# A fused transformer block on one core: first MLP's softplus as one table instruction, table sets in the planner, float32 products begun per head pair

## The chip, the cores and the metric

The kernel runs on 1 core of one Trainium2 chip. The time is the device time of one execution, in microseconds (us). Engines are named as in the profile: PE (TensorE matmul), PEld (its weight loads), DVE (VectorE), ACT (ScalarE), POOL (GpSimd), SP (SyncE, which issues the transfers).

## What is computed

Attention of q, k, v (4 batches, 8 heads, 576 rows, 64 columns), then two MLPs (512 to 2048 to 512) over all 2304 rows:

```python
out_d = sm_attn(q_d, k_d, v_d)                 # q, k, v averaged over 4 rows, 144 rows each
out_up = np.repeat(out_d, factor, axis=2)
mask = np.abs(pos[:, None] - pos[None, :]) < factor
attn = np.exp(scores); attn = attn / (np.sum(attn, axis=-1, keepdims=True) + 1e-09)
return (out_up + out_local).astype(np.float32)

h = x @ w_in                                   # first MLP
g = np.maximum(h, 0.0) + np.log1p(np.exp(-np.abs(h)))
return (g @ w_out).astype(np.float32)

h = x @ w_in                                   # second MLP
g = h * np.cos(h)
return (g @ w_out).astype(np.float32)
```

The weights arrive as float64. The first MLP's g is softplus(h).

## The kernel before

**Tiles.** Rows are cut into five token tiles, t = 0 to 4, of 512, 512, 512, 512 and 256 rows. The 2048 hidden columns are 16 features f of 128. Almost all products are float16 with three terms (high times high, high times low, low times high), so each operand is split into a high and a low half. Only tile 0 of the first MLP does its first F0 = 6 features otherwise: `first_in(f)` (from L1270) multiplies the float32 weights by the float32 attention output `raw0` .. `raw3` (one for each pair of heads, c = 0 to 3), at L1277; `first_out(f)` (L1300) multiplies the result by float32 w1o at L1314. Features 6 to 15 of tile 0 and all later tiles go through `unit_in` (L1327, matmuls at L1341), `rest_in` (L1424) and `l2` (matmuls at L1522). The second MLP's products stand at L1376 and L1572.

**Attention.** `pair(b, c)` (L739) does one batch and one pair of heads, sixteen in all. Its steps carry the names p<b><c> and a letter: sum1, sum2 (pooled q, k), sum3, sum4 (pooled v), A (scores), A2 and A3 (maximum, subtraction), A4 (exp, L852), B, B1, B1a, B2 (the same for the pooled scores; exps at L937), A5, N1, N2, A6, B4 (sums, reciprocals, scaling; B4 is one DVE instruction), C, C0, C1, D, D1 (transposes and their copies by ACT), E (products with v), up, E1 (the sum, written to `raw` or to `xt`).

**Weights.** `Weight.decode` (load, rebase by ACT L636 with Prelu, join1 and join2 by DVE L480 and L644), `bound` (ACT L666, Abs with an accumulator), `fit` (a maximum over partitions by a PE transpose and DVE) and `split` (high by ACT L495 or DVE, low by DVE L491) turn a block of two features into float16 halves.

**Softplus before.** Per unit of a feature: ACT takes Abs (L1438) and Relu (L1442) of the product in PSUM, Exp (L1446), Ln (L1450); DVE adds them (step G, L491), then step gh copies to float16 (ACT L501 or DVE L503) and step gl takes the rest (DVE L483). In `first_in` it is Abs, Exp, Ln (L1286, L1290, L1294) and the DVE step G (L1298).

**Order.** All steps are put in a `Plan`. `order()` runs a list scheduler over five queues: of the steps that are ready, the one due first goes to a free engine; due times come from a backward pass, plus the hand-fitted offsets of the table MOVES. Each engine then executes in exactly that order. Where the planner has no PE work it issues matmuls of zeros (`filler`, L1850), which keep PE running. PSUM is four two-bank slots (`any`); `halve(0, ...)` turns one of them into two one-bank slots `h`, which `first_in` and `unit_in` write to. In the kernel before it does so after the last of the first four pairs:

```python
        for b, c in pairs[:4]:
            pair(b, c)
...
        halve(0, outs_of[3:])
```

## Time and profile before

| | |
|---|---|
| median of 3 runs (lowest, highest) | 847.86 us (846.75 to 848.07) |
| span of the profiled execution | 847.6 us, 0.26 us below that median |
| PE busy | 834.0 us, 98% of the span |
| DVE busy | 719.1 us, 85% |
| ACT busy | 533.6 us, 63% |
| mean granted PE clock | 0.998 |
| HBM | 53.85 MB read, 4.72 MB written |

The profiled execution is told by its span alone, from its first to its last instruction. Busy times are averages over stages: what binds is read stage by stage, and PE counts as busy with its matmuls of zeros too. A duration in a row contains a tail that the next instruction of the engine overlaps; where work is added up, the distance from start to start is used.

### The profile page before, as it was taken

Reading aid. Unit: us, or ns where it says so; the run is one execution under the profiler, and the core shown is the slowest. Engines: PE = TensorE matmul, PEld = TensorE weight load, DVE = VectorE, ACT = ScalarE, POOL = GpSimd, SP = SyncE. Lnnn points to the kernel's source line nnn. Section 1 sums busy time; section 2 is a strip of 40 time slices with the busy share of each in tenths; the row PEclk is TensorE's granted clock in tenths of the full one; section 3 lists DMA queues with packets and bytes.
Section 4 is the critical chain, followed back from the end, with each engine's and each line's share of the span. In section 5 each row is a group of like instructions: output and inputs, shape, how many; then the busy total and the mean of one; then the engine's idle time right before and its main releaser. Section 6 shows DMA issues by size and latency. Waiting matters only on the chain.

```text
span 847.6 us, 15741 instructions
## 1 busy us (share of the span) xinstructions
PE 834.0 (98%) x6325; PEld 493.8 (58%) x6325; DVE 719.1 (85%) x1482; ACT 533.6 (63%) x964; POOL 1.8 (0%) x9
## 2 busy tenths in 40 slices
PE   8988999999999999999999999999999999999998
PEld 4634545455545555444467886676666565676664
DVE  7989999997767858999968999998779679889763
ACT  5478996686635747699977876556444335555441
POOL 0000000000000000000000000000000000000000
PEclk9999999999999999999999999999999999999999
DMA  9876441112110300342023200000000100100010
GB/s 321 281 277 240 162 173 41 51 33 64 61 45 1 117 1 2 120 178 100 1 99 107 94 2 1 1 1 29 23 1 1 51 1 1 51 1 2 2 50 25
DMA packets 14361, 59.57 MB, mean 70 GB/s; under 512 B 1681, under 2 KB 1809, under 8 KB 10193
## 3 DMA queue, kind: packets, MB, share of 16 engines
q1 hardware_dynamic: 14288, 58.58, 19.9%
q8 instruction: 49, 0.80, 0.4%
q14 instruction: 24, 0.19, 0.1%
HBM read 53.85 MB, written 4.72 MB: 69 GB/s over the span
## 4 chain that ended last, share of the span: by engine, by line
PE 89%; ACT 5%; DVE 3%; DMA 2%; issue 0%; POOL 0%; POOLq 0%; ACTq 0%; SPq 0%
PE any L1572 22%; PE h L1376 20%; PE any L1522 19%; PE h L1341 19%; PE any L1314 1%; PE any L1097 1%; PE any L1850 1%; DMA stg<-w1o 1%; PE any L817 1%; PE any L972 1%; PE h L1277 1%; DMA stg<-w1i 1%; ACT w1i_t L636 1%; ACT w1i_t L495 0%; DVE w1i_t L644 0%; ACT ed L937 0%
## 5 line engine op out<-in xcount | busy, mean ns | idle before, releaser
L1572 PE MATMUL any<-w1i_t,g 128*128 128x512 f16 x864 | 197.8, 379 | 0.5 <-DVE w1o_t L497 0.5
L1341 PE MATMUL h<-xt,w1i_t 128*128 128x512 f16 (+1 forms) x888 | 179.5, 356 | 0.1
L1376 PEld LDWEIGHTS <-w2i_t 128*128 128x128 f16 x1536 | 150.2, 98 | 31.6 <-issue 0.3
L1522 PE MATMUL any<-g,w1o_t 128*128 128x512 f16 (+1 forms) x792 | 157.2, 353 | 0.0
L1572 PEld LDWEIGHTS <-g 128*128 128x128 f16 x864 | 84.5, 98 | 88.4 <-issue 1.1
L1341 PEld LDWEIGHTS <-w1i_t 128*128 128x128 f16 x888 | 86.1, 98 | 83.0 <-issue 2.6
L1522 PEld LDWEIGHTS <-w1o_t 128*128 128x128 f16 x888 | 85.7, 98 | 79.9 <-issue 1.4
L483 DVE TENSOR_TENSOR g<-td,g 128x512 f16<-128x512 f32 (+1 forms) x146 | 92.0, 630 | 8.9 <-ACT g L501 6.0
L1376 PE MATMUL h<-xt,w2i_t 128*128 128x256 f16 x720 | 94.3, 273 | 0.1
L1474 ACT ACTIVATE tc<-ta 128x512 f32<-128x512 f32 (+1 forms) x80 | 46.8, 585 | 66.7 <-DVE ta L483 64.6
L1376 PE MATMUL h<-w1o_t,w2i_t 128*128 128x256 f16 x624 | 78.9, 273 | 0.0
L501 ACT ACTIVATE g<-td 128x512 f16<-128x512 f32 (+1 forms) x81 | 48.4, 598 | 38.8 <-DVE td L1478 28.1
L1463 ACT ACTIVATE ta<-hs,quarter,i 128x512 f32<-128x512 f32 x64 | 51.5, 808 | 30.2 <-DVE hs L483 29.6
L1438 ACT ACTIVATE ta<-h,i 128x512 f32<-128x512 f32 (+1 forms) x74 | 47.1, 637 | 25.7 <-PE h L1341 21.4
L1478 DVE SCALAR_TENSOR_TENSOR td<-hs,r,tc 128x512 f32<-128x512 f32 x64 | 48.0, 750 | 13.7 <-ACT tc L1474 12.5
L483 DVE TENSOR_TENSOR hs<-h,hs 128x512 f32<-128x512 f32 (+1 forms) x96 | 57.2, 598 | 2.4 <-PE h L1376 1.6
L483 DVE TENSOR_TENSOR ta<-ta,tb 128x512 f32<-128x512 f32 (+1 forms) x80 | 50.9, 636 | 1.4
L1442 ACT ACTIVATE tb<-h,r 128x512 f32<-128x512 f32 (+1 forms) x74 | 47.1, 636 | 5.9 <-PE h L1341 4.0
L1450 ACT ACTIVATE ta<-ta,one 128x512 f32<-128x512 f32 (+1 forms) x74 | 49.8, 675 | 1.4
L491 DVE SCALAR_TENSOR_TENSOR td<-ta,sg,tb 128x512 f32<-128x512 f32 (+1 forms) x64 | 43.6, 682 | 7.8 <-ACT ta L1450 6.8
L1468 DVE TENSOR_SCALAR tb<-ta 128x512 f32<-128x512 f32 (+1 forms) x80 | 31.8, 398 | 17.1 <-ACT ta L1463 16.3
L1446 ACT ACTIVATE ta<-ta 128x512 f32<-128x512 f32 (+1 forms) x74 | 43.1, 585 | 0.3
(198 smaller groups left out, 1045.1 us busy)
## 6 DMA issues: line engine op xcount, KB each, us to landing
qk<-qk SPq DMA_DIRECT2D x16, 589.0 KB, 5.9
stg<-w1i SPq DMA_DIRECT2D x8, 1024.0 KB, 6.0
stg<-w1o SPq DMA_DIRECT2D x8, 1024.0 KB, 5.0
stg<-w2i SPq DMA_DIRECT2D x8, 1024.0 KB, 4.9
stg<-w2o SPq DMA_DIRECT2D x8, 1024.0 KB, 4.7
vw<-vw SPq DMA_DIRECT2D x16, 320.0 KB, 5.5
out<-w1o_t SPq DMA_DIRECT2D x18, 256.0 KB, 2.0
vd<-vd SPq DMA_DIRECT2D x8, 288.0 KB
```

Of the source, the lines that this page charges most:

```text
L483: eng[e].tensor_tensor(out=out, in0=in0, in1=in1, op=op)
L501: nc.scalar.activation(out=out, in_=in_, func=AF.Copy)
L1341: nc.tensor.matmul(h.t[:, 0:n], l, r, start=(i == 0), stop=(i == 11))
L1376: nc.tensor.matmul(h.t[:, a : a + 256], l, r, start=(i == 0), stop=(i == n - 1))
L1438: act(n, 1, True), lambda: nc.scalar.activation(out=a(), in_=h.t[:, 0:n], func=AF.Abs, scale=col(o.i1, f)),
L1442: act(n, 1, True), lambda: nc.scalar.activation(out=b(), in_=h.t[:, 0:n], func=AF.Relu, scale=col(o.r1, f)),
L1450: act(n, 1), lambda: nc.scalar.activation(out=a(), in_=a(), func=AF.Ln, bias=one),
L1463: act(n, 2, psum), lambda: nc.scalar.activation(out=a(), in_=h.t[:, a0 : a0 + n], func=AF.Identity, scale=col(o.i2, f), bias=quarter), [h, ...
L1474: act(n), lambda: nc.scalar.activation(out=r(), in_=a(), func=AF.Sin, scale=TWOPI),
L1478: dve(n, False, 1), lambda: nc.vector.scalar_tensor_tensor(out=td.t[:, 0:n], in0=h.t[:, a0 : a0 + n], scalar=col(o.r1, f), in1=r(), op0=AL ...
L1522: nc.tensor.matmul(a.t[:, i, 0:n], l, r, start=(first and j == 0), stop=(last and j == 2))
L1572: nc.tensor.matmul(a.t[:, i], l, r, start=(f == 0 and j == 0), stop=(f == NF - 1 and j == 2))
```

## The change

- **Softplus.** `first_in` does one ACT instruction Softplus from PSUM, which writes g; Abs, Exp, Ln and the DVE step G are gone. In `rest_in` of the first MLP one Softplus takes the place of Abs, Relu, Exp, Ln and G; gh and gl read its float32 result and apply the factor `sg` themselves (gl becomes a DVE scalar_tensor_tensor at L493 of the changed kernel). Its results use the two buffers `ta` and the two `tb` in turn.
- **Attention's exps.** From the fifth pair on (BASE = 4) A4 and B2 use Softplus with -20 added to the argument; the sums of a row are scaled alike, so the factor cancels. N1's constant follows.
- **Tables.** Steps carry the table set that they need. The planner adds 1.3 us where the set changes (LOAD), and lets a step of another set wait until it is 4 us overdue against the others (HOLD). In the built program ACT holds 56 table loads; before, 2.
- **B4** of the first four pairs is three ACT instructions in place of one DVE instruction.
- **Float32 products.** The products of features 0 to 3 (before: 0 and 1) are cut into four parts, one for each pair of heads, and `halve(0, ())` now stands ahead of the first four pairs. So these have three two-bank slots, and two one-bank slots exist from the start.
- MOVES is fitted anew, for the whole program. Matmuls of zeros: 75 before, 65 now. All other matmuls are the same in number and shape.

```diff
+PF = 4
-PARTS = 2
+PARTS = 4
+SETS = {"": ("ex", "sp", "tr"), "ex": ("ex",), "sp": ("sp",), "tr": ("tr",), "pr": ("ex", "tr")}
+LOAD, HOLD = 1.3, 4.0
+BASE, LOWER = 4, 20.0
...
-    "L1 0 0": -32.5, "L1 0 10 exp#1": 38.5, "L1 0 10 gl#1": 66, "L1 0 10 mm#1": 57, "L1 0 11 abs#1": 73,
+    "L1 0 0": -406, "L1 0 0 mm#1": -404, "L1 0 1": -3265, "L1 0 10 mm#1": -32, "L1 0 11": -34, "L1 0 11 gl#1": 151.5,
...
+            held, started, late = set(), False, None
+            for op in [*ready, None]:
+                if op is None or late and free["act"] <= now and op.due > late.due + HOLD:
+                    if not late:
+                        break
+                    op = late
...
+                if e == "act" and loaded not in SETS[op.table] and op is not late:
+                    if late is None:
+                        late = op
+                    held.update(want)
+                    continue
...
+                    if e == "act" and loaded not in SETS[op.table]:
+                        end, loaded = end + LOAD, SETS[op.table][0]
...
+                P.add(act(1144), rebase, [raw], [x], [], nm + " rebase", over, "pr")
...
+            joint, dense, small, below = i >= XAB, i >= XD, i >= XE, i >= BASE
+            power, table = (AF.Softplus, "sp") if below else (AF.Exp, "ex")
...
+                kw = {"bias": lower} if below else {}
+                nc.scalar.activation(out=sm.t, in_=sm.t if i >= PX else scores(), func=power, scale=0.125, **kw)
...
+                if below:
+                    nc.scalar.activation(out=nd.t, in_=nd.t, func=AF.Identity, scale=float(2.0**-7), bias=lower)
+                else:
+                    nc.scalar.activation(out=nd.t, in_=nd.t, func=AF.Copy, scale=float(2.0**-7))
...
-            aop({"dve": 0.52 + 0.06 * small}, B4, [r], [ed], [], nm + "B4")
+            if i < PF:
+                for t in range(3):
+                    aop(act(SD, 1), lambda t=t: scaled("act", row(t), row(t), r.t[:, 2 * NG + t : 2 * NG + t + 1]), [r], [ed], [], nm + "B4")
+            else:
+                aop({"dve": 0.52 + 0.06 * small}, B4, [r], [ed], [], nm + "B4")
...
-            h, ta, g = HB.new(), TA.new(), GS.new()
+            h, g = HB.new(), GS.new()
...
-            P.add(
-                act(512, 0, True), lambda: nc.scalar.activation(out=ta.t, in_=h.t, func=AF.Abs),
-                [h], [ta], [ta], nm + "abs",
-            )
-            P.add(
-                act(512), lambda: nc.scalar.activation(out=ta.t, in_=ta.t, func=AF.Exp, scale=-1.0),
-                [], [ta], [], nm + "exp",
-            )
             tables.append(P.add(
-                act(512, 1), lambda: nc.scalar.activation(out=ta.t, in_=ta.t, func=AF.Ln, bias=one),
-                [], [ta], [], nm + "ln",
+                act(512, 0, True), lambda: nc.scalar.activation(out=u.g(), in_=h.t, func=AF.Softplus),
+                [h], [g], [g], nm + "soft", table="sp",
             ))
-            P.add(
-                dve(512, False, 1), lambda: nc.vector.scalar_tensor_tensor(
-                    out=u.g(), in0=h.t, scalar=0.0, in1=ta.t, op0=ALU.max, op1=ALU.add
-                ), [h, ta], [g], [g], nm + "G",
-            )
...
-            ta, tb, td, g = TA.new(), TB.new(), TD.new(), None
+            ta, td = (TA, TB)[k == 1 and f % 2].new(), TD.new()
             sc = [("sc", t) if (k, t) != (1, 0) else "sc0"]
-            a, b = lambda: ta.t[:, 0:n], lambda: tb.t[:, 0:n]
+            a = lambda: ta.t[:, 0:n]
             if k == 1:
-                P.add(
-                    act(n, 1, True), lambda: nc.scalar.activation(out=a(), in_=h.t[:, 0:n], func=AF.Abs, scale=col(o.i1, f)),
...
-                    act(n, 1, True), lambda: nc.scalar.activation(out=b(), in_=h.t[:, 0:n], func=AF.Relu, scale=col(o.r1, f)),
-                    [h, *sc], [tb], [tb], nm + "relu",
-                )
-                P.add(
-                    act(n), lambda: nc.scalar.activation(out=a(), in_=a(), func=AF.Exp, scale=-1.0),
-                    [], [ta], [], nm + "exp",
-                )
                 tables.append(P.add(
-                    act(n, 1), lambda: nc.scalar.activation(out=a(), in_=a(), func=AF.Ln, bias=one),
-                    [], [ta], [], nm + "ln",
+                    act(n, 1, True), lambda: nc.scalar.activation(out=a(), in_=h.t[:, 0:n], func=AF.Softplus, scale=col(o.i1, f)),
+                    [h, *sc], [ta], [ta], nm + "soft", table="sp",
...
-                P.add(
-                    dve(n, False, 1), lambda: mix(
-                        "dve", td.t[:, 0:n], a(), col(sg, f), b(), ALU.add
-                    ), [ta, tb, *sc], [td], [td], nm + "G",
-                )
+                v, x, sg = ta, a, o.sg if t else o.lc
...
-            P.add(
-                {**act(n), **dve(n, True)}, lambda e: copy(e, u.hi(), td.t[:, 0:n]),
-                [td], u.keys, u.claim, nm + "gh",
-            )
-            low = dve(n)
-            P.add(low, lambda: two("dve", u.lo(), td.t[:, 0:n], u.hi(), ALU.subtract), [td], u.keys, [], nm + "gl")
+            if k == 1:
+                high, low = (act(n, 1), dve(n, True, 1)), dve(n, False, 1)
+                up = lambda e: scaled(e, u.hi(), x(), col(sg, f))
+                down = lambda: less("dve", u.lo(), x(), col(sg, f), u.hi())
+            else:
+                high, low = (act(n), dve(n, True)), dve(n)
+                up = lambda e: copy(e, u.hi(), x())
+                down = lambda: two("dve", u.lo(), x(), u.hi(), ALU.subtract)
+                sc = []
+            P.add({**high[0], **high[1]}, up, [v, *sc], u.keys, u.claim, nm + "gh")
+            P.add(low, down, [v, *sc], u.keys, [], nm + "gl")
...
-        for b, c in pairs[:4]:
-            pair(b, c)
-
...
-        halve(0, outs_of[3:])
-
+        halve(0, ())
+        for b, c in pairs[:4]:
+            pair(b, c)
```

**PE, at the end of the first four pairs.** any is a two-bank PSUM slot, h a one-bank slot; zero marks the matmuls of zeros, raw0 to raw3 are the attention outputs of tile 0, L1277 (now L1288) a part of a float32 product. Before:

```order
L1097 MATMUL any1_85<-aT1_130,vw0_115 64x58 x16
...
L1277 MATMUL h0_756<-raw0_161,w1i_t_159 128x512
...
L817 MATMUL any0_84<-qk1_111 64x64 x20
L890 MATMUL any0_84<-qd0_119 64x144 x4
L896 MATMUL h1_757<-qd0_119 64x144 x2
L1277 MATMUL h0_756<-raw1_162,w1i_t_159 128x512
L1277 MATMUL h0_756<-raw2_163,w1i_t_159 128x512
L1277 MATMUL h0_756<-raw3_164,w1i_t_159 128x512
L1277 MATMUL h1_757<-raw0_161,w1i_t_159 128x512
```

Now, from the transposes of pair 02 (L1019) on; L1108 is a pair's product with v, first 02's and then 03's (before: L1097):

```order
L1019 MATMUL any1_85<-ident_73,ed0_127 72x128 x6
L1288 MATMUL h1_281<-raw0_161,w1i_t_159 128x512
...
L1108 MATMUL any0_84<-aT0_129,vw2_117 64x58 x16
...
L1288 MATMUL h1_281<-raw1_162,w1i_t_159 128x512
...
L1019 MATMUL any1_85<-ident_73,ed1_128 72x128 x6
L1288 MATMUL h1_281<-raw2_163,w1i_t_159 128x512
...
L1108 MATMUL any0_84<-aT1_130,vw0_115 64x58 x16
...
L1288 MATMUL h0_280<-raw0_161,w1i_t_159 128x512
...
L1288 MATMUL h0_280<-raw1_162,w1i_t_159 128x512
L1288 MATMUL h1_281<-raw3_164,w1i_t_159 128x512
L1288 MATMUL h0_280<-raw2_163,w1i_t_159 128x512
```

The first part of a float32 product stood behind pair 03's product with v, and pair 10's scores (L817 to L896) behind that part; now the parts of raw0 to raw2 stand between the steps of pairs 02 and 03, two parts of a second product follow, and pair 10's scores come after both.

**ACT, at the first Softplus instructions.** L1297 (now) is Softplus of a float32 product, L944 and L856 the exps of pair 10, L638 Prelu of a weight block. Before:

```order
L937 ACTIVATE ed0_127,rs_0_230<-any0_84,nd_0_234 128x144
L1286 ACTIVATE ta0_94<-h0_756 128x512
L852 ACTIVATE sm1_125<-sm1_125 128x640
L1290 ACTIVATE ta0_94<-ta0_94 128x512
L636 ACTIVATE w1i_t_159<-stg1_109 128x1024
L1294 ACTIVATE ta0_94<-ta0_94,one_78 128x512
L1286 ACTIVATE ta1_95<-h1_757 128x512
L1290 ACTIVATE ta1_95<-ta1_95 128x512
L1294 ACTIVATE ta1_95<-ta1_95,one_78 128x512
```

Now:

```order
L638 ACTIVATE w1i_t_159<-stg1_109 128x1024
L1297 ACT_TABLE_LOAD
L1297 ACTIVATE g0_100<-h1_281 128x512
L1297 ACTIVATE g1_101<-h0_280 128x512
L638 ACT_TABLE_LOAD
L638 ACTIVATE w1i_t_159<-stg0_108 128x1024
L937 ACTIVATE nd_0_234<-nd_0_234,lower_78 128x3
L944 ACT_TABLE_LOAD
L944 ACTIVATE ed0_127,rs_0_230<-any2_89,nd_0_234 128x144
L944 ACTIVATE ed0_127,rs_0_230<-h1_281,nd_0_234 128x144
L944 ACTIVATE ed0_127,rs_0_230<-any2_89,nd_0_234 128x144
L856 ACTIVATE sm1_125<-sm1_125,lower_78 128x640
```

Three instructions per float32 product became one, and three table loads stand among the twelve rows.

**PE, ahead of the first float16 product of tile 0** (L1341, now L1339, reading xt0). L1314 (now L1312) is the float32 product of `first_out`; x2 is one half d of it, two matmuls; L817 and L890 are scores of pair 12. Before, two halves stand ahead of it:

```order
L1314 MATMUL any1_85<-g0_100,w1o_t_160 128x512 x2
...
L817 MATMUL any0_84<-qk0_110 64x64 x20
L890 MATMUL any0_84<-qd0_119 64x144 x4
L896 MATMUL h0_756<-qd0_119 64x144 x2
L1314 MATMUL any1_85<-g1_101,w1o_t_160 128x512 x2
...
L1341 MATMUL h1_757<-xt0_79,w1i_t_159 128x512
```

Now seven:

```order
L1312 MATMUL any1_85<-g1_101,w1o_t_160 128x512 x2
...
L1312 MATMUL any2_89<-g1_101,w1o_t_160 128x512 x2
L1312 MATMUL any1_85<-g0_100,w1o_t_160 128x512 x2
L1312 MATMUL any2_89<-g0_100,w1o_t_160 128x512 x2
L1312 MATMUL any1_85<-g2_102,w1o_t_160 128x512 x2
L1312 MATMUL any2_89<-g2_102,w1o_t_160 128x512 x2
...
L1312 MATMUL any2_89<-g4_104,w1o_t_160 128x512 x2
...
L1339 MATMUL h0_280<-xt0_79,w1i_t_159 128x512
```

Five more halves, ten matmuls, stand ahead of the first float16 product than before.

## Rows read from the trace of the kernel before

**Rows 1.** The page, part 1: busy us, share of the span and instructions by engine.

```profile
PE 834.0 (98%) x6325; PEld 493.8 (58%) x6325; DVE 719.1 (85%) x1482; ACT 533.6 (63%) x964; POOL 1.8 (0%) x9
```

**Rows 2.** Windows: stretch, length, busy (instructions) of PE, PEld, DVE, ACT, POOL; PEclk, DMA.

```profile
0.00:45.40 45.40, 42.48 (x621) 25.59 (x622) 39.28 (x76) 22.91 (x61) 1.77 (x9) 1.00 0.89 301
45.40:83.39 37.99, 32.84 (x241) 15.55 (x239) 33.81 (x71) 29.86 (x57) 0.00 (x0) 0.96 0.70 250
83.39:103.22 19.83, 19.37 (x130) 9.87 (x129) 19.34 (x33) 19.77 (x39) 0.00 (x0) 1.00 0.48 173
...
340.00:400.00 60.00, 60.00 (x286) 27.46 (x284) 59.03 (x130) 50.36 (x76) 0.00 (x0) 1.00 0.39 131
400.00:500.00 100.00, 99.42 (x711) 68.75 (x710) 88.29 (x176) 82.80 (x150) 0.00 (x0) 1.00 0.20 70
...
804.00:847.60 43.60, 39.42 (x243) 23.45 (x240) 20.61 (x54) 13.84 (x29) 0.00 (x0) 0.99 0.10 37
```

**Rows 3.** Windows of line L1850 alone, the matmuls of zeros (PE, PEld).

```profile
0.00:45.40 45.40, 19.59 (x69) 6.37 (x69) 1.00 0.89 301
45.40:83.39 37.99, 1.62 (x6) 0.54 (x6) 0.96 0.70 250
```

**Rows 4.** PE's timeline: start, length, line, tiles, records [idle before <-releaser].

```profile
43.19 0.33 PE L811 MATMUL any<-mask_sb,ident_b 64*64 64x320 bf16 x4
...
44.52 2.84 PE L1277 MATMUL h<-raw,w1i_t 128*128 128x512 f32 x6
48.14 3.70 PE L1277 MATMUL h<-raw,w1i_t 128*128 128x512 f32 x8 [0.77 <-ACT ed L937]
53.81 5.40 PE L1277 MATMUL h<-raw,w1i_t 128*128 128x512 f32 x8 [1.97 <-DVE g L1298]
59.04 0.71 PE L972 MATMUL any<-ident,sm 128*128 128x128 f32 x5
...
83.39 2.75 PE L1341 MATMUL h<-xt,w1i_t 128*128 128x512 f16 x12
...
105.81 1.88 PE L1314 MATMUL any<-g,w1o_t 128*128 128x512 f32 x4
107.53 0.82 PE L1008 MATMUL any<-ident,ed 128*72 128x128 f32 x6
```

**Rows 5.** Groups by line and shape: busy, mean ns | idle before, releaser; DVE.

```profile
L1298 DVE SCALAR_TENSOR_TENSOR g<-h,ta 128x512 f32<-128x512 f32 x6 | 4.1, 690 | 2.6 <-ACT ta L1294 2.6
L483 DVE TENSOR_TENSOR ed<-ed,rs 128x432 f32<-128x432 f32 x8 | 4.8, 600 | 0.0
L491 DVE SCALAR_TENSOR_TENSOR td<-ta,sg,tb 128x512 f32<-128x512 f32 x48 | 35.9, 748 | 7.1 <-ACT ta L1450 6.8
```

**Rows 6.** The same view, ACT.

```profile
L1286 ACT ACTIVATE ta<-h 128x512 f32<-128x512 f32 x6 | 3.5, 588 | 1.7 <-PE h L1277 1.7
L1290 ACT ACTIVATE ta<-ta 128x512 f32<-128x512 f32 x6 | 3.8, 625 | 0.1
L1294 ACT ACTIVATE ta<-ta,one 128x512 f32<-128x512 f32 x6 | 4.3, 720 | 0.1
...
L1438 ACT ACTIVATE ta<-h,i 128x512 f32<-128x512 f32 x58 | 39.7, 684 | 25.1 <-PE h L1341 21.4 <-DVE td L491 2.7 <-DVE am L1217 0.7
```

**Rows 7.** ACT's timeline around the two table loads.

```profile
0.73 1.28 ACT L462 ACT_TABLE_LOAD   x1 [0.73 <-PEq L1928]
2.36 0.31 ACT L464 ACTIVATE ident_s<-ident 128x128 bf16<-128x128 f32 x1 [0.35 <-POOL ident masks.py:199]
...
495.16 0.81 ACT L1463 ACTIVATE ta<-hs,quarter,i 128x512 f32<-128x512 f32 x1 [0.57 <-DVE hs L483]
495.99 1.28 ACT L1474 ACT_TABLE_LOAD   x1
498.24 0.63 ACT L1474 ACTIVATE tc<-ta 128x512 f32<-128x512 f32 x1 [0.97 <-DVE ta L483]
```

More of the change, by code (lines that the diff above doesn't have):

```diff
@@ L180, in __init__, with add @@
         self.ops, self.wrote, self.read, self.time = [], {}, {}, {}
-    def add(self, cost, fn, reads=(), writes=(), claim=(), name="", after=()):
-        op = Op(len(self.ops), cost, fn, claim, name)
+    def add(self, cost, fn, reads=(), writes=(), claim=(), name="", after=(), table=""):
+        op = Op(len(self.ops), cost, fn, claim, name, table)
         pre = set(after)
@@ L289, in order @@
                 ready.append(op)
-        now, busy, dma_free = 0.0, [], 3.7
+        now, busy, dma_free, loaded = 0.0, [], 3.7, "ex"
         ready.sort(key=lambda o: (o.due, o.n))
@@ L312, in order @@
                         want[v.slots] = want.get(v.slots, 0) + 1
-                if any(s in held or len(s.free) < m for s, m in want.items()):
+                if op is not late and any(s in held or len(s.free) < m for s, m in want.items()):
                     held.update(want)
@@ L430, in build @@
         quarter = const.tile([128, 1], F32, name="quarter")
-        one = const.tile([128, 1], F32, name="one")
+        lower = const.tile([128, 1], F32, name="lower")
         xt = [const.tile([128, NC_, n], F32, name=f"xt{t}") for t, (_, n) in enumerate(TILES)]
@@ L467, in build @@
         nc.vector.memset(quarter, 0.25)
-        nc.vector.memset(one, 1.0)
+        nc.vector.memset(lower, -LOWER)
         for v in VD.tiles:
@@ L647, in join2 @@
                     )
-                P.add(act(1144), rebase, [raw], [x], [], nm + " rebase", over)
+                P.add(act(1144), rebase, [raw], [x], [], nm + " rebase", over, "pr")
                 P.add(dve(1024, True), join1, [], [x], name=nm + " join1")
@@ L672, in bound @@
                     act(1024, 1), total, [("float", self.name, b), free], [("bd", self.name, b), *held],
-                    name=f"{self.name}{b} bound",
+                    name=f"{self.name}{b} bound", table="pr",
                 )
@@ L726, in build, with aop @@
         stages = {}
-        def aop(cost, fn, reads=(), writes=(), claim=(), name=""):
-            stage = name.split()[-1]
-            op = P.add(cost, fn, reads, writes, claim, name, stages.get(stage, ()) if claim else ())
+        def aop(cost, fn, reads=(), writes=(), claim=(), name="", table=""):
+            stage = name.split()[-1].replace("qd", "sum1")
+            op = P.add(cost, fn, reads, writes, claim, name, stages.get(stage, ()) if claim else (), table)
             if claim:
@@ L851, in A4 @@
             def A4():
-                nc.scalar.activation(out=sm.t, in_=sm.t if i >= PX else scores(), func=AF.Exp, scale=0.125)
+                kw = {"bias": lower} if below else {}
+                nc.scalar.activation(out=sm.t, in_=sm.t if i >= PX else scores(), func=power, scale=0.125, **kw)
             def A5():
@@ L857, in N1 @@
             def N1():
-                nc.vector.tensor_scalar_add(r.t, r.t, 1e-9)
+                nc.vector.tensor_scalar_add(r.t, r.t, 1e-9 * float(np.exp(-LOWER)) if below else 1e-9)
             def N2():
@@ L937, in B2 @@
                     nc.scalar.activation(
-                        out=row(t), in_=src, func=AF.Exp, scale=float(2.0**-7),
+                        out=row(t), in_=src, func=power, scale=float(2.0**-7),
                         bias=nd.t[:, t : t + 1], accum_out=r.t[:, 2 * NG + t : 2 * NG + t + 1],
```

29 lines of the change are left out of this document (11 added, 18 removed), and 110 rows, old and new, of the table MOVES.

## The prediction

> **What bounds the kernel now.** I read the page first: PE is busy for 98% of the span [rows 1]. That alone is no bound, since matmuls of zeros count as busy. Then the windows: from 83.39 us on, where the first float16 product of tile 0 starts, PE misses 0.46 us up to 103 us, 0.58 us between 400 and 500 us and about 4 us at the end, though DVE is busy for 59.03 of 60 us in one stretch [rows 2]. Behind that point the kernel is as long as PE's own work, and this work is the same in both programs: all matmuls but those of zeros are equal in number and shape. So the change can win only what PE loses ahead of that point. There the windows and the row of the zeros show a lot: in the first 45.40 us 19.59 us of PE's 42.48 busy us are zeros [rows 2, 3], because DVE, busy for 39.28 us, feeds the attention pairs slowly; from 45.40 to 83.39 us PE is busy for 32.84 of 37.99 us, 1.62 of them with zeros, while DVE has 33.81 and ACT 29.86 us of work [rows 2, 3].
>
> **The loss ahead of the first float16 product.** I start where the first float32 product is done, at 47.4 us (the next one starts at 48.14 after 0.77 us of waiting [rows 4]), and go to 83.39 us: 36.0 us. PE's waits in it are what the window lacks in busy time, 37.99 - 32.84 = 5.15 us [rows 2], the longest of 1.97 and 0.77 us, for G on DVE and for an exp on ACT [rows 4]; the zeros take 1.6 us [rows 3]; and the product at 53.81 us lasts until 59.04, 5.2 us, where the one at 48.14 took 3.4 without its tail: after the wait of 1.97 us the clock was granted at the lower of its two levels, 1.2 GHz (the mean of this stretch is 0.96, of those around it 1.00 [rows 2]), a loss of 1.8 us. Lost: 5.15 + 1.6 + 1.8 = 8.5 us; own work: 36.0 - 8.5 = 27.5 us.
>
> **Parts of the change and their costs.**
>
> *Order of PE.* Five more halves of `first_out` stand ahead of the first float16 product. One half takes 1.72 us from start to start (105.81 to 107.53 us [rows 4]), so 8.6 us of work are done earlier. Up to the end of the first float32 product two parts of the second one are now done (0.86 us each, so -1.7 behind it), but pair 10's scores are not (+1.3 us, from 43.19 to 44.52 us in the old order [rows 4]). Behind that point PE then has 27.5 + 8.6 - 1.7 + 1.3 = 35.7 us of own work. The point itself hangs on pair 03's output, ahead of which DVE's order holds about as much work as before; I leave it at 47.4 us, and give it 2 us either way, since the pairs have three two-bank slots in place of four, but B4 leaves DVE.
>
> *The sum.* With L' for the loss that remains, the first float16 product starts at 47.4 + 35.7 + L' = 83.1 + L', with 8.6 us more done; against 83.39 us the span becomes 847.6 - 8.6 - 0.3 + L' = 838.7 + L'. A loss as before (8.5) would give 847.2, none 838.7. Everything hangs on L'.
>
> *DVE in this stretch.* Removed: six G of `first_in`, 4.1 us, and the 2.6 us that DVE waited for Ln ahead of them [rows 5]. In their place the order puts one more w1o block's joins, one more low half and a sixth pair's sums, so its work ahead of the point stays about 33.8 us, less 1.5 us that moved ahead of the start: 32.3 us. Before, that was more than PE's 27.5, by 6 of the 8.5 us lost; now PE has 35.7, and DVE is no bound by 3.4 us.
>
> *ACT in this stretch.* Removed: Abs, Exp, Ln of six products, 3.5 + 3.8 + 4.3 = 11.6 us [rows 6]. Added: six Softplus. No row shows one; the nearest is Abs from PSUM, 0.588 us [rows 6], the least an ACT pass over this tile took there, and a Softplus that is Exp and Ln in turn inside would take 0.625 + 0.720 = 1.35; I take 0.59, as the trace shows Exp and Ln within 0.14 us of a plain pass, so 3.5 us. Ten table loads stand here at 1.28 us [rows 7], 12.8 us. Sum: 29.9 - 11.6 + 3.5 + 12.8 = 34.6 us against PE's 35.7. ACT becomes nearly as long as PE.
>
> *Price of a switch.* The load at 495.99 us starts 0.02 us after the instruction ahead of it; 0.97 us lie between its end and the next instruction, but that waited for DVE; at the program's start 0.35 us lie behind a load, put down to POOL [rows 7]. So a switch costs between 1.28 and 2.25 us, and I take 1.28: the gap is explained by DVE's wait, and the nearest other row caps it at 1.63. The Trainium skill (ScalarE: Activation LUTs, section What ACT_TABLE_LOAD costs) gives 1283 ns for the load, as here, and 1380 ns more for a drain, 2.66 us for every switch. This trace shows no such drain ahead of a load; by the page the ten switches would be 26.6 us, and ACT's sum 48.4 us, which would make the change a loss.
>
> *L'.* Of the 8.5 us about 6 were DVE's and go. The rest, 2.5 us, is latency (waits for a pair's exps, for the maxima over partitions), which stays; with ACT full I add 0.5. L' = 3, so 841.7 us.
>
> *B4 on ACT*, four pairs: DVE loses 4 x 0.600 = 2.4 us [rows 5]; ACT gets 12 short instructions in a stretch in which it is busy for 22.91 of 45.40 us [rows 2]. Taken at nothing; the latency of a pair grows by some tenths.
>
> *Softplus in later units.* Per unit of 512 rows ACT does one pass of about 0.684 us [rows 6] in place of four, and DVE loses G, 0.748 us [rows 5]; 44 more loads cost 56 us of ACT over the whole. Nothing of this is on the path: PE misses half a microsecond per hundred there [rows 2], and ACT has 50.36 of 60 and 82.80 of 100 us now [rows 2]. If that cover went, a unit whose float16 halves come late would stop PE; up to eight g buffers stand between.
>
> **Rivals.**
>
> *The switch is dear (slower).* Between the first float32 product and the first use of a split feature of tile 0, `l2` of feature 6, the order has 17 loads against 76.6 us of PE work and 73.2 of ACT work at 1.28 us a load (an estimate: the order's instructions, each with the mean of its like in the trace): 3.4 us are spare. Each load that costs x more takes 17x - 3.4 us. At x = 0.97, the bound of [rows 7], that is 13.1, and 841.7 + 13.1 = 854.8 us; it cancels the gain of 5.9 from x = 0.55. For it: ACT has no room. Against it: 0.02 us ahead of one load, at most 0.35 behind the other. Chance 0.10. By the 2.66 us of the Trainium skill (ScalarE: Activation LUTs, What ACT_TABLE_LOAD costs) x would be 1.38 and the time 861.8; the two loads here do not bear it out.
>
> *The waits only change places.* In-order ACT holds a Prelu, then Softplus, then exps; one step that is late holds all behind it, the join of a weight block and the next pair among them. Then L' stays 8 to 9, and the time is 847.2, within 0.2%. For it: ACT's 34.6 of 35.7 us. Chance 0.10.
>
> *The first pairs suffer from three slots.* Each of the four pairs claims five slots in turn; if each waited 2 us longer for one, the first float32 product would end 8 us later: 841.7 + 8 = 849.7. DVE's 39.28 of 45.40 us leave little that could hide it. Chance 0.06.
>
> *It gains more*, L' near 0 and the pairs a little earlier as B4 leaves DVE: 836 to 838. Chance 0.08.
>
> **How the numbers follow.** The forecast, 841.7 us, has 0.66; its own range, from L' of 1 to 6 and the 2 us of the start, is 838 to 845.5. A measurement of this kernel tells about 0.2% from no change, 1.7 us, so same means 846.2 to 849.6. Faster: 0.66 + 0.08 + a small part of the second rival, 0.76. Same: the rest of that rival, 0.08. Slower: the dear switch and the slots, 0.16. The range takes in the gain, the forecast and the second rival and ends at the slots' 849.7; it leaves out the dear switch and some of the lowest times: 836 to 850. The profiled span is 0.26 us below the median; the forecast is 841.7 + 0.3 = 842 against 847.86.
>
> **What would show it.** Right: the first float16 product near 86 us with seven halves of `first_out` ahead of it; DVE idle between 47 and 86 us, ACT busy above 90%; PE's waits there for ACT more than for DVE; loads of 1.28 us with nothing behind them; 65 matmuls of zeros. Wrong: idle time of 0.5 us or more behind loads, or PE waits between 300 and 500 us (the switch); the float32 products late by several us (the slots); the first float16 product after 91 us (waits in new places).

## The result and the profile after

The changed kernel takes 854.84 us (median of 4 runs, 852.98 to 855.50) where the kernel before takes 847.54 beside it: 0.8% slower, ratio 1.008, 95% interval 1.0059 to 1.0101. Its profiled execution spans 853.1 us. The forecast was 842, the range ended at 850: wrong in sign and outside the range. In a later repeat on another chip (e0 below) it took 851.79 us, ratio 1.0045 (1.0028 to 1.0063); both say that the change costs time, and the loss is 0.45% to 0.8%.

The page of the changed kernel, parts 1 and 4 (the chain that ended last, by engine), answers to [rows 1]; the third line is part 4 of the kernel before:

```profile
PE 830.9 (97%) x6315; PEld 492.1 (58%) x6315; DVE 676.9 (79%) x1401; ACT 479.7 (56%) x788; POOL 1.8 (0%) x9
...
PE 81%; ACT 6%; DMA 6%; DVE 5%; issue 1%; POOL 0%; POOLq 0%; ACTq 0%; DVEq 0%; SPq 0%
...
PE 89%; ACT 5%; DVE 3%; DMA 2%; issue 0%; POOL 0%; POOLq 0%; ACTq 0%; SPq 0%
```

DVE and ACT have 42 and 54 us less to do, and the kernel is longer: less of its chain lies on PE. The windows, as in [rows 2]:

```profile
0.00:45.40 45.40, 38.51 (x521) 22.09 (x522) 36.86 (x72) 27.95 (x74) 1.77 (x9) 1.00 0.91 301
45.40:83.39 37.99, 33.91 (x283) 17.54 (x282) 29.87 (x63) 29.08 (x40) 0.00 (x0) 0.96 0.83 261
83.39:103.22 19.83, 18.27 (x119) 8.60 (x118) 16.49 (x24) 17.75 (x34) 0.00 (x0) 1.00 0.44 150
340.00:400.00 60.00, 60.00 (x287) 27.58 (x286) 58.10 (x126) 52.69 (x60) 0.00 (x0) 1.00 0.31 106
400.00:500.00 100.00, 98.05 (x683) 66.05 (x682) 75.22 (x170) 64.50 (x83) 0.00 (x0) 1.00 0.21 74
```

From 83 to 103 us PE now misses 1.56 us, where it missed 0.46; in the hundred from 400 us on 1.95, where it missed 0.58. The first float16 product starts at 91.10 us, with seven halves of `first_out` ahead of it. PE's longest waits from 47.7 to 150 us (engine, tile, line it waits at, releaser: us in total, times, longest):

```profile
PE h L523 <- ACT g L1297: 2.4, 1, 2.4
PE h L1288 <- ACT ed L944: 1.7, 1, 1.7
PE h L1339 <- DVE w1i_t L493: 1.6, 1, 1.6
PE any L1019 <- ACT aTd L503: 1.2, 1, 1.2
PE h L1339 <- ACT ta L1436: 0.8, 1, 0.8
PE h L523 <- ACT ta L1436: 0.4, 1, 0.4
```

Most of them end on ACT (L1297 and L1436 are Softplus, L944 attention's exps, L503 a copy). The longest of them, on ACT's timeline and then on PE's:

```profile
59.72 1.28 ACT L638 ACT_TABLE_LOAD   x1
62.18 1.13 ACT L638 ACTIVATE w1i_t<-stg 128x1024 f32<-128x1024 f32 x1 [1.17 <-DMA stg<-w1i]
65.33 1.06 ACT L668 ACTIVATE w1i_t<-w1i_t 128x1024 bf16<-128x1024 f32 x1 [2.02 <-DVE w1i_t L646]
66.29 0.19 ACT L668 ACTIVATION_READ_ACCUMULATOR w1i_t<-w1i_t 128x1 bf16 x1
66.39 0.63 ACT L503 ACTIVATE aTd<-any 72x576 f32<-72x576 f32 x1
67.02 1.28 ACT L1297 ACT_TABLE_LOAD   x1
68.31 0.60 ACT L1297 ACTIVATE g<-h 128x512 f32<-128x512 f32 x1
```

```profile
64.65 1.88 PE L1288 MATMUL h<-raw,w1i_t 128*128 128x512 f32 x4
68.96 0.38 PE L523 MATMUL h<-ident_s,bd_w1i 128*128 128x128 bf16 x4 [2.43 <-ACT g L1297]
```

A Prelu and an Abs of one weight block (L638, L668) stand ahead of a Softplus that frees PE's bank. Between Prelu and Abs ACT waits for DVE's joins, and around them stand two loads: PE's product is done at 66.5 us, and its Softplus starts at 68.31. Soon after this wait of 2.43 us the clock was granted at the lower of its two levels for a while (mean 0.66 from 70 to 75 us), which in e0, below, with 1.3 us of waiting at the same place, it was not:

```profile
70.00:75.00 5.00, 5.00 (x50) 2.69 (x51) 3.94 (x8) 4.95 (x7) 0.00 (x0) 0.66 0.44 130
```

```profile
70.00:75.00 5.00, 4.95 (x32) 1.97 (x34) 4.24 (x11) 4.97 (x7) 0.00 (x0) 1.00 0.68 214
```

### The profile page after: what moved, and what is told of

It is laid out like the page before. It is cut to its first block, busy times and chain, and to the rows that moved or that the text cites. A ratio compares the mean times of both kernels' runs of the same rounds, so it can differ in the third digit from the quotient of the medians.

```text
span 853.1 us, 15442 instructions
## 1 busy us (share of the span) xinstructions
PE 830.9 (97%) x6315; PEld 492.1 (58%) x6315; DVE 676.9 (79%) x1401; ACT 479.7 (56%) x788; POOL 1.8 (0%) x9
## 4 chain that ended last, share of the span: by engine, by line
PE 81%; ACT 6%; DMA 6%; DVE 5%; issue 1%; POOL 0%; POOLq 0%; ACTq 0%; DVEq 0%; SPq 0%
PE any L1558 21%; PE h L1374 19%; PE h L1339 18%; PE any L1508 18%; DMA vd<-vd 2%; DMA stg<-w1i 2%; PE any L1108 1%; DVE w1i_t L646 1%; ACT w1o_t L638 1%; DMA stg<-w1o 1%; DMA stg<-w2o 1%; DVE sm L485 1%; PE any L820 1%; PE any L983 1%; ACT w1i_t L668 1%
## 5 line engine op out<-in xcount | busy, mean ns | idle before, releaser
L1558 PE MATMUL any<-w1i_t,g 128*128 128x512 f16 x864 | 200.2, 379 | 1.1 <-DVE w1o_t L499 1.1
L1339 PE MATMUL h<-xt,w1i_t 128*128 128x512 f16 (+1 forms) x888 | 180.7, 356 | 2.5 <-DVE w1i_t L493 1.6
L1508 PE MATMUL any<-g,w1o_t 128*128 128x512 f16 (+1 forms) x792 | 160.2, 353 | 0.0
L1339 PEld LDWEIGHTS <-w1i_t 128*128 128x128 f16 x888 | 85.8, 98 | 86.4 <-issue 3.7
L503 ACT ACTIVATE g<-td 128x512 f16<-128x512 f32 (+1 forms) x58 | 35.3, 609 | 39.3 <-DVE td L1459 33.8
L485 DVE TENSOR_TENSOR g<-td,g 128x512 f16<-128x512 f32 (+1 forms) x80 | 50.5, 631 | 4.5 <-ACT g L503 2.8
L1459 DVE SCALAR_TENSOR_TENSOR td<-hs,r,tc 128x512 f32<-128x512 f32 x64 | 47.7, 746 | 7.7 <-ACT tc L1455 6.9
L1436 ACT ACTIVATE tb<-h,i 128x512 f32<-128x512 f32 (+1 forms) x37 | 23.5, 639 | 48.3 <-PE h L1339 39.8
L1436 ACT ACTIVATE ta<-h,i 128x512 f32<-128x512 f32 (+1 forms) x37 | 23.6, 640 | 31.2 <-PE h L1339 30.4
L1288 PE MATMUL h<-raw,w1i_t 128*128 128x512 f32 x48 | 24.1, 638 | 2.0 <-ACT ed L944 1.7
L1374 PE MATMUL h<-tx,w2i_t 128*128 128x256 f16 x192 | 24.1, 273 | 0.0
```

What stands on the lines that cost most here:

```text
L485: eng[e].tensor_tensor(out=out, in0=in0, in1=in1, op=op)
L503: nc.scalar.activation(out=out, in_=in_, func=AF.Copy)
L1288: nc.tensor.matmul(h.t, W1I.f32(f, 128 * c, 128), raw0[c], start=(c == 0), stop=(c == NC_ - 1))
L1339: nc.tensor.matmul(h.t[:, 0:n], l, r, start=(i == 0), stop=(i == 11))
L1374: nc.tensor.matmul(h.t[:, a : a + 256], l, r, start=(i == 0), stop=(i == n - 1))
L1436: act(n, 1, True), lambda: nc.scalar.activation(out=a(), in_=h.t[:, 0:n], func=AF.Softplus, scale=col(o.i1, f)),
```

## Experiments

All kernels below are the changed kernel in its own order; only what is named differs. Each is timed against the kernel before on the same chip (846 to 852 us there). To see where time goes I use four marks on PE: M1, the last matmul of the second float32 product; M2, the first float16 matmul of tile 0; M3 and M4, the 101st and the 201st of these. Each length is the difference of two start times in the trace (the last one's, of the end). The medians are of 4 to 12 runs, the lengths of one profiled execution each. e1, e2, e3, e10, e11 and e14 leave softplus out in whole or in part: they measure time and compute something else.

| run | median, us | ratio (95%) | M1 to M2 | M2 to M3 | M4 to end |
|---|---|---|---|---|---|
| changed, profiled above | 854.84 | 1.0080 (1.0059 to 1.0101) | 40.11 | 41.73 | 660.78 |
| e0 changed, again | 851.79 | 1.0045 (1.0028 to 1.0063) | 36.65 | 41.51 | 660.99 |
| e1 no switch | 845.58 | 0.9950 (0.9935 to 0.9965) | 34.75 | 37.51 | 660.81 |
| e2 no early switch | 846.07 | 0.9965 (0.9945 to 0.9984) | 34.74 | 37.51 | 662.79 |
| e3 no late switch | 851.84 | 1.0025 (1.0009 to 1.0040) | 36.64 | 41.42 | 661.19 |
| e4 B4 on DVE | 853.71 | 1.0042 (1.0029 to 1.0055) | 38.88 | 41.43 | 660.91 |
| e5 third staging buffer | 851.54 | 1.0034 (1.0022 to 1.0046) | 36.64 | 41.62 | 660.69 |
| e6 Exp and Ln | 848.32 | 0.9998 (0.9983 to 1.0012) | 35.50 | 38.09 | 661.33 |
| e7 e6 and B4 on DVE | 851.24 | 1.0027 (1.0013 to 1.0042) | 35.08 | 38.09 | 661.43 |
| e8 Exp and Ln early only | 848.15 | 0.9998 (0.9987 to 1.0008) | 35.97 | 38.13 | 662.88 |
| e9 MLP's switches | 852.80 | 1.0050 (1.0034 to 1.0065) | 37.76 | 39.96 | 662.45 |
| e10 attention's switches | 850.48 | 1.0028 (1.0013 to 1.0043) | 36.46 | 39.75 | 660.67 |
| e11 plain passes, 1.22 us | 850.92 | 1.0023 (1.0008 to 1.0039) | 36.01 | 39.85 | 661.18 |
| e12 e8, order at 480 us | 846.99 | 0.9969 (0.9954 to 0.9985) | 35.09 | 38.07 | 660.32 |
| e13 changed, order at 480 us | 850.59 | 1.0026 (1.0012 to 1.0040) | 38.85 | 40.54 | 660.31 |
| e14 plain passes, 1.41 us | 851.79 | 1.0032 (1.0018 to 1.0047) | 36.48 | 41.30 | 662.72 |

**Is it the switches?** Theory S says that the table loads in ACT's queue make the loss; rival O, that the new order does.

```diff
-power, table = (AF.Softplus, "sp") if below else (AF.Exp, "ex")
+power, table = (AF.Exp, "sp") if below else (AF.Exp, "ex")
-nc.scalar.activation(out=u.g(), in_=h.t, func=AF.Softplus)
+nc.scalar.activation(out=u.g(), in_=h.t, func=AF.Relu)
-nc.scalar.activation(out=a(), in_=h.t[:, 0:n], func=AF.Softplus, scale=col(o.i1, f))
+nc.scalar.activation(out=a(), in_=h.t[:, 0:n], func=AF.Relu, scale=col(o.i1, f))
```

(These are e1's lines.) In e2 the first of them and the last read differently, and in e3 only the last is changed:

```diff
+power, table = (AF.Softplus if i >= 8 else AF.Exp, "sp") if below else (AF.Exp, "ex")
+nc.scalar.activation(out=a(), in_=h.t[:, 0:n], func=AF.Softplus if t else AF.Relu, scale=col(o.i1, f))
```

```diff
+nc.scalar.activation(out=a(), in_=h.t[:, 0:n], func=AF.Relu if t else AF.Softplus, scale=col(o.i1, f))
```

> The changed kernel in its own order, with Exp for Softplus in attention and Relu for Softplus in the first MLP (so the softplus is left out): 2 table loads in place of 56, all other instructions, their order and waits equal. Theory S, the table loads hold ACT's queue between 49 and 127 us and so PE: the 18 loads ahead of 152 us cost 23 us of ACT, and the time falls to 842 to 846 us. Rival O, the new order itself loses (transfers and latencies that stand late in it, with or without loads): 850 us or more.

> As before, but only ahead of 147 us: Exp in the attention pairs 4 to 7, Relu in tile 0 of the first MLP (its softplus is left out); the later pairs and tiles keep Softplus and their 36 or so loads. Theory S says that nearly all of the loss is made ahead of 150 us: 1 to 3 us above the run without any switch, 844 to 849. If the late loads count as well, 848 to 852. Rival O: 850 or more.

> The converse: Softplus and loads as in the changed kernel up to tile 0, Relu in tiles 1 to 4 (their softplus is left out), so some 35 loads behind 320 us are gone. Theory S (early loads) and rival O both say little: 852 to 854.5. If late loads make up a good part of the loss (PE's wait of 2 us at 486 and the small ones behind it), 849 to 851.

Measured: S. Without switches the same order is 0.5% faster than the kernel before; 0.45% to 0.8% slower with them. An exp takes as long as a Softplus of the same shape (0.412 us at L944 in e0 and in e1), so it is the loads that were taken away. Nearly all of it is early: e2 has e1's lengths up to M3, and e3 has e0's. From M4 on, e1 with one load and e0 with 36 are equal (660.81 and 660.99 us), so late loads cost nothing that shows; what e2 has more there (662.79) goes with PE's clock at 480 us, below. The windows of e0, then of e1 (columns as above):

```profile
47.00:88.00 41.00, 38.96 (x312) 19.18 (x310) 34.99 (x74) 37.06 (x55) 0.00 (x0) 1.00 0.77 271
88.00:130.00 42.00, 38.66 (x311) 19.64 (x309) 33.62 (x68) 36.58 (x57) 0.00 (x0) 1.00 0.34 115
```

```profile
47.00:88.00 41.00, 40.62 (x360) 20.82 (x359) 37.35 (x77) 25.24 (x47) 0.00 (x0) 1.00 0.82 292
88.00:130.00 42.00, 41.22 (x326) 21.15 (x324) 35.79 (x74) 29.84 (x57) 0.00 (x0) 1.00 0.37 129
```

With loads ACT is busy for 90% and 87% of the stretches and PE misses 5.4 us in them; without, 62% and 71%, and PE misses 1.2. PE's waits of 47 to 130 us in e1 are three, of 0.8 us at most:

```profile
PE h L1339 <- ACT ta L1436: 0.8, 1, 0.8
PE h L1288 <- DVE w1i_t L646: 0.2, 1, 0.2
PE h L523 <- ACT g L1297: 0.2, 1, 0.2
```

**The other edits.** B4 as one DVE instruction, and a third staging buffer:

```diff
-aop(act(SD, 1), lambda t=t: scaled("act", row(t), row(t), r.t[:, 2 * NG + t : 2 * NG + t + 1]), [r], [ed], [], nm + "B4")
+aop(act(SD, 1), lambda t=t: scaled("act", row(t), row(t), r.t[:, 2 * NG + t : 2 * NG + t + 1]), [r], [ed], [], nm + "B4").whole = (B4, t)
...
+if hasattr(op, "whole"):
+    op.fn = op.whole[0] if op.whole[1] == 0 else lambda: None
```

```diff
+STG.tiles.append(W1O.t[:, 12288:16384].bitcast(I64).rearrange("p (m e) -> p m e", m=2))
+mine = [v for op in ops if op.name[:2] == "w1" and op.name.endswith("load") for v in op.claim]
+for i, v in enumerate(mine):
+    v.i = i % 3 if i < 9 else (i - 9) % 2
```

> The changed kernel in its own order, but B4 of the first four pairs again as one DVE instruction, at the place of the first of the three ACT instructions. If B4 on ACT is what delays the first pairs: 3 us or more lower than the changed kernel, 851 or less, with pair 03's output earlier. If it is worth nothing either way (theory S and rival O): 853.5 to 856.

> The changed kernel in its own order, with a third staging buffer for its first nine weight blocks (it lies in the part of w1o's tile that blocks 6 and 7 fill later), so a load no longer waits for the join of the block two ahead. If the late weight loads (ACT waits 2.5, 1.17 and 1.12 us for them behind a table load) are a cause of their own: 3 us or more below the changed kernel, 0.4% or more. Theory S, ACT's queue with its table loads sets the pace: under 2 us, 0.2%.

> The changed kernel itself, beside the others on the same chip, as the base for them: 0.6% to 1.0% above the kernel before.

e0 itself came out below its expectation, at 0.45%. Against e0 both edits are without effect in the time (their intervals overlap e0's). So late weight loads are no cause of their own: a third buffer leaves both stretches as they are, 36.64 and 41.62 us.

**Softplus without a switch.** Exp and Ln of 1 + e lie in one set with Prelu and Abs: e6 needs 2 table loads in all. e6 calls this for every unit, with Exp in attention (the line of e1); e7 has e4's edit besides; e8 calls it where t is 0, with the attention line of e2.

```diff
+def soft(out, h, **kw):
+    nc.scalar.activation(out=out, in_=h, func=AF.Exp, **kw)
+    nc.scalar.activation(out=out, in_=out, func=AF.Ln, bias=one)
```

> The changed kernel in its own order, but softplus as Exp and Ln of 1 + e (two ACT instructions, one table set with Prelu and Abs), and Exp in attention: 2 table loads, complete computation. ACT pays some 0.65 us more per unit than in the run without any switch, but no load. Theory S: within 2 us of that run, so 0.2% to 0.5% below the kernel before (845 to 848 us where that takes 849). If ACT's busy time as such is what binds, the Ln costs what the loads did in the early stretch: no faster than the kernel before.

> The same with B4 of the first four pairs as one DVE instruction. In the run with loads this was worth some 0.3%. If that gain came from a shorter queue on ACT ahead of the first table loads, little of it is left here: within 1 us of the run with Exp and Ln. If it came from the latency of a pair: 2 to 3 us below that run.

> The changed kernel in its own order; ahead of 147 us no table is switched: Exp in pairs 4 to 7, and tile 0's softplus as Exp and Ln of 1 + e; the later pairs and tiles keep Softplus and their 37 loads. Complete computation. Theory S (only the early loads cost; the late ones lie beside PE's work): as the run without early switches, plus at most 1 us for the Ln, so 0.25% to 0.4% below the kernel before (846 to 847 us where that takes 849.2). If the late loads or the Ln cost something: no faster than the kernel before.

Up to M3 most of the loss disappears (e6 73.59 us, e1 72.26, e0 78.16), but neither e6 nor e8 is faster than the kernel before, where theory S had expected 0.2% to 0.5% less. e6 gives 1.3 us away between M3 and M4 (60.87 us, in e1 59.53), where tile 1's Ln and the last two of tile 0 stand. e8 has only these two there and gives 0.75 us away (60.28); it loses another 2 us behind 470 us (662.88, e1 660.81), which again goes with the clock there. e7 was expected at or below e6 and is 2.9 us above it, 12 runs each and intervals apart: with ACT's queue short, B4 on ACT does gain. The place is the first pairs: DVE writes raw0 and raw1 11.77 us apart in e6 and 12.81 in e7 (rows below), and 11.77 in e0 and 12.81 in e4. So B4 on ACT gains 1.0 us with loads too; there the time does not show it.

```profile
24.47 0.68 DVE L1138 TENSOR_TENSOR raw<-any,up 128x512 f32<-128x512 f32 x1
...
36.24 0.68 DVE L1138 TENSOR_TENSOR raw<-any,up 128x512 f32<-128x512 f32 x1
```

```profile
21.84 0.68 DVE L1138 TENSOR_TENSOR raw<-any,up 128x512 f32<-128x512 f32 x1
...
34.65 0.69 DVE L1138 TENSOR_TENSOR raw<-any,up 128x512 f32<-128x512 f32 x1
```

Much of the rest of the 2.9 us goes with PE's clock: it was at its lower level for a while in e7's profile (mean 0.66 from 44 to 49 us, 1.00 in e6), and over the whole run its mean was 0.998 or less in 8 of e7's 12 runs and in 3 of e6's. The medians of the other runs are 849.3 and 848.3. What lowers the clock more often in e7 was not tried.

**Which part's switches?**

> The changed kernel in its own order with Exp in pairs 4 to 7, Softplus in the first MLP: the loads that are left early are tile 0's (56 in all, as many as before, since a load goes ahead of an exp and another comes ahead of the next Softplus). If tile 0's Softplus among the weight blocks' Prelu and Abs makes the loss: as the changed kernel, 0.3% to 0.6% above the kernel before. If attention's Softplus does: as the run without early switches, 0.2% or more below.

> The converse: Softplus in attention and in tiles 1 to 4, Relu in tile 0 (its softplus is left out): 9 early loads in place of 18. If tile 0's switches make the loss: 0.1% to 0.35% below the kernel before. If attention's do: 0.3% or more above it. If every load costs about alike: in the middle between the run without early switches and the changed kernel, within 0.15% of the kernel before.

e9 is the changed kernel with the attention line of e2 alone, e10 with the Relu lines of e2 alone (in `first_in`, and in `rest_in` where t is 0). From M1 to M3 they take 77.72 and 76.21 us: 5.5 and 4.0 us above e1, together more than the 5.9 of e0. But the two are no halves. e9 still has 14 loads between M1 and M3, where e0 has 16, since each Softplus of tile 0 now stands between steps of the other set; so e9 tells only that these loads cost about what the average of e0's does, 0.39 us each. e10 has 6 loads there, and they cost 0.66 us each, though ACT is busy for only 56.4 of 76.2 us:

```profile
49.18:125.40 76.22, 72.19 (x606) 36.52 (x604) 65.21 (x132) 56.37 (x95) 0.00 (x0) 1.00 0.58 191
```

Both lose 1.4 to 1.6 us more between M3 and M4 (61.10 and 60.96 us), where they have loads of attention (at 132.5 and 128.0 us) that e0 does not have. So either part alone makes most of the loss; the costs do not add, and what a load costs depends on where it stands.

**What does a load cost?** In e11 and e14 (no early switch) two plain passes stand where the 18 early loads stood.

```diff
+held, pads = "ex", 0
...
+if op.eng == "act" and held not in SETS[op.table] and pads < 18:
+    held, pads = SETS[op.table][0], pads + 1
+    for _ in range(2):
+        nc.scalar.activation(out=pad, in_=quarter.to_broadcast([128, PAD]), func=AF.Copy)
...
```

> The run without early switches (Exp in pairs 4 to 7, Relu in tile 0, whose softplus is left out), with two plain passes on a scratch tile, some 1.25 us together, at the place of each of the 18 early loads. If a load costs no more than the time for which it occupies ACT: as the changed kernel, 0.3% to 0.6% above the kernel before. If a switch holds up more than that (the dear switch of the prediction): clearly lower than the changed kernel, within 0.2% of the kernel before or below it.

> The plain passes at the places of the 18 early loads again, but longer: the load takes 1.41 us from the end of one instruction to the start of the next where two instructions overlap by 0.10, the two passes took 1.22; now some 1.41. If a load costs just the time for which it keeps ACT: from the 16th float32 matmul to the 101st float16 matmul of tile 0 some 78 us, as with the loads (78.2; 75.9 with the shorter passes, 72.3 with none), and 0.3% to 0.6% above the kernel before. If a switch costs something besides: 76 us or less.

In e0 the median of the 55 loads behind the first is 1.313 us from the end of the instruction ahead to the start of the one behind, where two plain instructions overlap by some 0.10 (their tail): a load keeps ACT for 1.41 us. With `PAD` of 536 and 650 columns that gap is 1.125 and 1.315 us. The same instructions in e11 and in e14 (duration min/median/max, first and last start):

```profile
L1853 ACT ACTIVATE pad<-quarter x36: 631/648/668, 48.9 to 145.4; 128x536 bf16<-128x536 f32 x36
```

```profile
L1853 ACT ACTIVATE pad<-quarter x36: 727/744/763, 48.6 to 147.6; 128x650 bf16<-128x650 f32 x36
```

e11 loses 3.6 us against e1 from M1 to M3 (75.86 less 72.26), e14 5.5, e0 5.9; e14 has e0's lengths in both stretches within 0.2 us. So a load costs as much as other work that keeps ACT that long in the same place, and a switch has no further price that shows. ACT's busy time between these marks against the loss:

| | e1 | e10 | e6 | e11 | e9 | e0 | e14 |
|---|---|---|---|---|---|---|---|
| ACT busy, us | 48.4 | 56.4 | 57.7 | 67.0 | 67.8 | 69.5 | 69.7 |
| M1 to M3, us | 72.3 | 76.2 | 73.6 | 75.9 | 77.7 | 78.2 | 77.8 |

The loss begins long before the sums of the two engines are equal. But the sum does not set it: e10, with less work on ACT than e6, loses three times as much (4.0 against 1.3 us), and e9 with hardly more than e11 loses 5.5 against 3.6. In e6 the added work stands at tile 0's softplus, in e10 around attention's exps. Which step behind each load is the one that PE then waits for was not tried load by load.

**The wait at 480 us.** In e0 PE waits 2.2 us at L523, the transposes of w2o's last bounds (470 to 500 us; the kernel before waits 0.5 us at its L521 there):

```profile
PE h L523 <- ACT stg L668: 2.2, 2, 1.3
```

The wait is the order's and not the late loads': e1, without them, has 1.8 us of it. In e2, e8, e9 and e14 more is lost behind M4. In these four the clock was granted at its lower level right after this wait, in the other profiles it was not. Windows of e8, of e2 and of e0 (e9 and e14 have 0.91 from 475 to 495 us as well):

```profile
480.00:484.00 4.00, 3.99 (x21) 2.79 (x22) 4.00 (x26) 1.15 (x1) 0.00 (x0) 0.57 0.00 0
```

```profile
475.00:495.00 20.00, 18.22 (x151) 15.15 (x149) 16.75 (x57) 9.80 (x14) 0.00 (x0) 0.91 0.00 1
```

```profile
475.00:495.00 20.00, 17.84 (x164) 15.63 (x162) 18.08 (x59) 11.13 (x16) 0.00 (x0) 1.00 0.11 45
```

M4 to the end takes 662.5 to 662.9 us in the four and 660.7 to 661.4 in the other profiles with this order: the lower clock costs some 1.7 us (an estimate, the difference of the two means). e12 and e13 change the order at 480 us:

```diff
...
+ahead([("L1 4 12 gl", 1432), ("L1 4 13 gl", 1438)], ("w2o5 low", 1453))
+ahead([("L2 4 14 0", 1585), ("L2 4 14 1", 1586), ("L2 4 12 0", 1558),
+       ("L2 4 12 1", 1559), ("L2 4 13 0", 1560), ("L2 4 13 1", 1561)], ("wmax spread", 1476))
```

> The run with Exp and Ln in tile 0 (no early switch, complete), and at 480 us one piece of the order changed: six groups of tile 4's output matmuls, and the two DVE steps that two of them need, go ahead of the transposes of w2o's bounds, for which PE waited 2.2 us there. If that wait is a loss of its own, behind and apart from the early switches: 2 us less than that run, 0.2% to 0.35% below the kernel before, and this version is faster than both. If the chain of w2o only stops PE a little later: no difference, within 0.1% of the kernel before.

> The changed kernel with that piece of the order alone, switches as they are. If the late loss is apart from the early one: 1 to 2 us below the changed kernel, 0.2% to 0.5% above the kernel before, and from the first product of the second MLP on as many us as in the changed kernel. If not: 0.45% or more above.

The wait at L523 is gone in both; part comes back at 488 us (waits of e12, 470 to 500 us):

```profile
PE h L1380 <- DVE hs L491: 1.2, 1, 1.2
PE h L1380 <- ACT pu L1408: 0.3, 1, 0.3
```

M4 to the end takes 660.3 us in both, 0.7 less than e0 and, with the clock kept, 2.6 less than e8; of these 2.6 some 1.7 are the clock's. e13 is still slower than the kernel before, e12 is faster than the kernel before and than the changed kernel: 0.9969 (0.9954 to 0.9985). It computes everything, with 38 loads, all but the first of them behind 147 us.

## Why the prediction was wrong

The profiled span is 853.1 against 841.7 forecast, 11.4 us more. The step that failed by most is "behind that point the kernel is as long as PE's own work": from the first float16 product on it takes 6.4 us more than forecast, 4.2 of them where seven loads in ACT's in-order queue hold PE up. The other 5.0 us are the start (2.3) and L' (2.7). By the prediction's own steps:

- *The start, 47.4 us:* failed by 2.3 us. By the order shown ahead, the part with raw3 that completes the first float32 product comes third from 46.80 us on, so the product is done at 49.70 us (two parts of 0.86 behind 47.98). Its input raw3 is written by DVE from 47.47 us on, before from 43.95:

```profile
46.80 1.12 PE L1288 MATMUL h<-raw,w1i_t 128*128 128x512 f32 x2
...
47.98 3.60 PE L1288 MATMUL h<-raw,w1i_t 128*128 128x512 f32 x8
```

```profile
47.47 0.67 DVE L1132 TENSOR_TENSOR raw<-any,up 128x512 f32<-128x512 f32 x1
```

```profile
43.95 0.69 DVE L1121 TENSOR_TENSOR raw<-any,up 128x512 f32<-128x512 f32 x1
```

  In the runs with B4 on ACT the product is done between 47.8 us (e3) and 51.8 (e1), and from the end of raw0 to that of raw3 pass 23.9 to 25.4 us, with switches and without, where the kernel before took 20.1. So pairs 01 to 03 do suffer in the new order, by less than the rival of three slots had (8 us). Whether for the slots or for the new order of steps was not tried, and stays open. It is not B4: taken at nothing, its move to ACT gains 1.0 us (e4, e7).
- *L' = 3:* 91.10 - 49.7 - 35.7 = 5.7 us in the profiled run, so +2.7. In e0 it is 87.90 - 50.0 - 35.7 = 2.2, without switches 0.3 (e1: 87.86 - 51.8 - 35.7; e2 the same). PE's own work was sized well: it is busy for 35.66 us of this stretch in e1 and 35.89 in e0. The latency that stays, 2.5 us, was too much by 2.2, and the switches add 1.9 where I had 0.5; that the two nearly cancel in e0 is luck. The other 3.5 us of the profiled run are not shown to be the change's: PE is busy 1.4 us longer there with the same matmuls, at the lower clock from 70 us on, and waits 2.0 us more; a transfer took longer (below). The stretch in the profiled run, e0 and e1:

```profile
49.70:91.10 41.40, 37.31 (x302) 18.47 (x301) 33.13 (x68) 34.20 (x51) 0.00 (x0) 0.96 0.80 256
```

```profile
49.97:87.90 37.93, 35.89 (x301) 17.72 (x300) 31.92 (x68) 34.24 (x51) 0.00 (x0) 1.00 0.76 271
```

```profile
51.82:87.86 36.04, 35.66 (x302) 17.72 (x301) 32.39 (x68) 22.61 (x43) 0.00 (x0) 1.00 0.81 287
```

- *ACT full, yet no bound:* this step failed, 1.9 us for 0.5. ACT's 34.6 of PE's 35.7 us came out near the trace (34.2 us in e0). In-order ACT, with waits for DVE and for transfers between its instructions, loses PE time well below 100%: in e10 at 74%.
- *"Behind that point the kernel is as long as PE's own work":* this step failed by more. Behind the first float16 product it takes 762.0 us (853.1 - 91.1; in e0 as well) where 755.6 were forecast. 4.2 of these 6.4 us lie between M2 and M3 (41.73, in e1 37.51), where seven of the loads stand that I priced at nothing. The row spoke against it: from 83.39 to 103.22 us ACT was busy for 19.77 of 19.83 us already [rows 2]; I read only PE's 0.46 us there. The other 2.2 are the new order's: mostly the wait at 480 us, and two shorter ones at 582 and 746 us, which e1 has as well.
- *Softplus and loads in later units at nothing:* right from M4 on (e3, e1).
- *Softplus at 0.59 and 0.684 us:* right, 0.601 and 0.686 in the trace.
- *Price of a switch, 1.28 us:* near. The load takes 1.283 us, starts 0.018 us behind the instruction ahead and ends 0.012 before the next, in most places; counted with the tails that it parts, 1.41. The Trainium skill (ScalarE: Activation LUTs, What ACT_TABLE_LOAD costs) gives 1380 ns more for a drain; no load here shows it, neither in these gaps nor in the time of e0 against e14.
- *The median from the span:* I added 0.3 us. Each run's time is some 1.8 us above its span (854.94 against 853.1 us in the profiled run), so the execution of 847.6 us that all sums start from was slower than the median one; by this 842 was 1.5 us low, apart from the mechanism.

*The rivals.* The dear switch gave the time, 854.8 us, but not the mechanism: x was 0.13 in place of 0.97, and by its own formula, 17x - 3.4, nothing would have been lost. "The waits only change places" had the right reason (one late step holds all behind it in ACT's queue), but not the place: it had L' at 8 to 9, where 5.7 and in e0 2.2 were measured, and its total of 847.2 was too low because it left the start where it was and stopped at the first float16 product. Of the signs that I named, the right ones came as well (65 zeros, ACT at 90% in e0 though at 82% from M1 to M2 in the profiled run, PE's waits more for ACT than for DVE, nothing behind most loads) as three of the wrong ones: the first float16 product after 91 us in the profiled run, the float32 products late by 2.3 us, and waits of PE between 400 and 500 us, which are not the loads' (e1 has them). A sign that agrees with two stories tells little.
